# The first unit's expert is chosen before the last unit is routed, and its rows are turned before the table of the others

## The chip, the cores and the metric

The kernel runs on one core of one Trainium2 chip. The time is that of the whole program in device microseconds, the median of the runs shown. The core's engines are TensorE (PE in the rows, with its weight loads as PEld), VectorE (DVE), ScalarE (ACT), GpSimd (POOL) and SyncE (SP), which only starts transfers and reads values. SP and ACT each have a queue of transfers (SPq and ACTq in the rows), and POOL a third one, for transfers whose row numbers come from a tile.

## The reference

Three networks follow each other. An attention over 32 memory slots per head gives 4608 rows of 512. A router sends each row to one of 8 experts, and the expert's result, weighted by the router's probability, is the input of a last dense network.

```python
attn_out = _attn_ref(q, k, v, phi)                      # (8, 8, 576, 64)
x = attn_out.transpose(0, 2, 1, 3).reshape(4608, 512)
logits = x @ w_gate + modality_bias[modality_id]
e_idx = np.argmax(logits, axis=1)
# ... softmax over the logits; gate_w is the probability of the expert taken
for e in range(8):
    mask = e_idx == e
    h = np.maximum(x[mask] @ w1[e], 0.0)                # w1: 512 x 1024
    out[mask] = gate_w[mask, None] * (h @ w2[e])        # w2: 1024 x 512
h = out @ w_in                                          # 512 x 2048
g = np.maximum(h, 0.0) + np.log1p(np.exp(-np.abs(h)))
return g @ w_out                                        # 2048 x 512
```

How many rows an expert gets is known only while the program runs.

## The kernel before

**Attention and routing** (attention_and_routing). The 4608 rows are 18 units of 256 rows. A unit's scores, softmax and values give its rows and router logits. `route` takes the largest logit, and `rank` counts, with matmuls by a triangular matrix, which place each row gets within its expert's region of the array `xs` in memory; the running counts are in `base`. POOL then scatters the rows into `xs`, 128 at a time (L449). Units go to `rank` in pairs, but the last two, 16 and 17, go alone. On each engine the order of this part is made by the framework's scheduler.

**Two choices.** `choose(0)` runs after unit 9 and picks the expert that has the most rows by then; 256 of its rows are read back and computed among the rest of the attention (`chosen`, L481). `choose(1)` runs after the last `rank`: it picks the expert with the most rows left, and 512 of its rows become unit 0 of the expert stage. Both put the expert's number and its first row into the tile `few` (L459, L462), which SP and ACT read with a value load.

**The table** (`listed`, twice, L586 to L643). Some sixty small VectorE instructions on one partition turn the counts into the list of the other units: expert, first row, place of the result. It follows `choose(1)` in the code.

**The expert stage** (experts) is in an order written out by hand. Its head is L746 to L770. ACT starts the first quarter of both weight matrices of unit 0 as soon as the expert is known (L749). SP and ACT start the reading of the 512 rows into `raw` (L752), two transfers each. SP then starts the rest of the weights, the gates `ig` and the first piece of the last network's weights (`convert_in(0)`, tile `d`). `part(0, 0)` and `part(0, 1)` split the first weights into a high and a low half (ACT writes the high one, VectorE the low one), and four calls of `turn` each transpose a quarter of the rows (VectorE) and split it (ACT and VectorE) into `hl`. The unit's loop of 8 steps follows. Step n is 12 matmuls of layer 1 (`hidden_of`, tile `ph`), a relu on ACT and VectorE (`h`, L125 and L126), the splits of weights that later steps need, and 12 matmuls of layer 2, two steps behind. The rows of the unit after it are read into the same `raw` (`rows_of(1)`, by a value of the table) and turned in steps 3 and 4.

What a pool of tiles leaves free when it closes is given to pools that open later. An instruction that writes such a tile waits for everything that used the memory before.

Of the kernel before, what the change touches and what calls it, by code (L numbers as in the profile page):

```python
# [9 lines left out]
F32 = mybir.dt.float32  # L10
# [9 lines left out]
P = 128  # L20
# [3 lines left out]
UNITS = TILES // 2  # L24
DM = H * D
E, F = 8, 1024
FF = 2048
FC = F // P
# [49 lines left out]
def full(tc, *reads):  # L78

    for w in reads:  # L80
        tc.add_to_no_dep_group("full", w.ins)
# [56 lines left out]
def tile_kernel(ctx, tc, qT, kv, phi, mid, wg, mbias, w1, w2, wffn, out):  # L138
# [21 lines left out]
    rows = ExitStack()  # L160
    ps_y = rows.enter_context(tc.tile_pool(name="ps_y", bufs=2, space=PSUM, side="right"))
    ig0 = cst.tile([P, 2, 2], F32, name="ig0")
    weights, py0 = attention_and_routing(tc, locals())
    act = ctx.enter_context(tc.tile_pool(name="act", bufs=1))
    raw = act.tile([P, UNIT // 32, P], F32, name="raw")
# [3 lines left out]
    ids = [act.tile([P, BLK // P], I32, name=f"ids{j}") for j in range(2)]  # L169
    idf = act.tile([P, BLK // P], F32, name="idf")  # L170
    ps_3 = ctx.enter_context(tc.tile_pool(name="ps_3", bufs=2, space=PSUM))
    begun = experts(tc, locals())
    rows.close()
    last_network(tc, locals())
# [2 lines left out]
def attention_and_routing(tc, env):  # L177
    nc = tc.nc
    V, A, G, PE, SP = nc.vector, nc.scalar, nc.gpsimd, nc.tensor, nc.sync
    qT, kv, phi, mid, wg, mbias, w1, w2 = (env[n] for n in ("qT", "kv", "phi", "mid", "wg", "mbias", "w1", "w2"))  # L180
    xs, table, nslots, pick, ig0, ps_y, K, Q, J = (
        env[n] for n in ("xs", "table", "nslots", "pick", "ig0", "ps_y", "K", "Q", "J"))

    with ExitStack() as st:
        pool = lambda name, bufs, **kw: st.enter_context(tc.tile_pool(name=name, bufs=bufs, **kw))
# [25 lines left out]
        iota_i = c.tile([P, TILES], I32, name="iota_i")  # L211
        G.iota(iota_i, pattern=[[P, TILES]], base=0, channel_multiplier=1)
        desc = c.tile([P, E], F32, name="desc")
        base = [c.tile([P, E], F32, name=f"base{i}") for i in range(2)]
        zero_base = c.tile([P, E], F32, name="zero_base")
        for e in range(E):
            G.memset(desc[:, e:e + 1], float(E - e))
            G.memset(base[0][:, e:e + 1], float(e * RG + PAD))
            G.memset(zero_base[:, e:e + 1], float(e * RG + PAD))
        ids = c.tile([P, TILES], F32, name="ids")  # L220
        V.tensor_copy(ids, iota_i)
        zero = c.tile([P, ROW], F32, name="zero")
# [11 lines left out]

        W = Expert(nc, env)
        cnt = [c.tile([1, E], F32, name=f"cnt{i}") for i in range(3)]
        past = [zero_base[0:1], *(c.tile([1, E], F32, name=f"past{i}") for i in range(2))]
        most = c.tile([1, 2], F32, name="most")
        raw0 = lt.tile([P, SLOT // 32, P], F32, name="raw0")
        apart = ["xs"]  # L240
# [185 lines left out]
        def rank(gi):  # L426
# [19 lines left out]
            V.reciprocal(xr[:, 0:n, DM + 1], gs)  # L446
            V.scalar_tensor_tensor(xr[:, 0:n, DM], ri, 0.0, ids[:, t0:t0 + n], op0=ALU.mult, op1=ALU.add)
            for i in range(n):
                once(G.indirect_dma_start(xs, IndirectOffsetOnAxis(ap=ri[:, i:i + 1], axis=0), xr[:, i, :], None,  # L449
                                          bounds_check=E * RG - 1, oob_is_err=False))  # L450

        def choose(i, rows):

# [99 lines left out]
        for u in range(UNITS):  # L553
            if u == 0:
                load(2)
            point(4 * u)
            if u + 2 < UNITS:
                scores(u + 2)
            if u in (0, 2, 5, 7, 9):
                load(3 + (0, 2, 5, 7, 9).index(u))  # L560
            point(4 * u + 1)
            values(u, 0)
            point(4 * u + 2)
            if u + 1 < UNITS:
                transp(u + 1)
            values(u, 1)
            if u and u - 1 == units[group[u - 1]][-1]:
                rank(group[u - 1])
                if u == CHOICE:
                    choose(0, base[(group[u - 1] + 1) % 2][0:1])  # L570
                    fetch()
            if u == units[group[u]][-1]:
                route(group[u])
            point(4 * u + 3)
            if u == CHOICE:
                steps = chosen()
            if u in PADS:
                for e in range(2 * (u - PADS[0]), 2 * (u - PADS[0]) + 2):
                    once(pad(SP, xs, zero, e))
            for i in range(STEPS.get(u, 0)):  # L580
                next(steps)
        rank(len(units) - 1)
        choose(1, base[len(units) % 2][0:1])


        last = base[len(units) % 2][0:1]  # L586
        I = lambda *s, n, dt=F32: c.tile([1, *s], dt, name=n)
        V.memset(table, 1)

# [51 lines left out]
        *_, n = listed(SLOT, MAXS, TABU, n_s, end_s, None)  # L641
        V.tensor_scalar(nslots, n, 1.0 / SLOT, float(SLOTS_E), op0=ALU.mult, op1=ALU.max)
        V.tensor_scalar(nslots, nslots, float(TABU), None, op0=ALU.add)  # L643
        for _ in steps:
            pass
    return W, *chosen_rows


def experts(tc, env):
# [5 lines left out]
    with ExitStack() as st:  # L655
# [87 lines left out]
            regs[s] = value(0, entry(s), E - 1), value(3, entry(s), 1)  # L743

        with tc.manual_schedule():
            head = lambda w, eng, hi: eng.value_load(pick[1][:, w:w + 1], min_val=0, max_val=hi)  # L746
            ea, x0 = head(0, A, E - 1), head(1, SP, E * RG - UNIT)
            for w in range(2):
                load(w, 0, ea, eng=A)  # L749
            xa = head(1, A, E * RG - UNIT)  # L750
            for x, eng, js in ((x0, SP, (0, 1)), (xa, A, (2, 3))):
                full(tc, *rows_in(nc, eng, raw, xs[ds(x, UNIT)], UNIT, js))  # L752
            e0 = head(0, SP, E - 1)
            for w in range(2):
                load(w, 1, e0)
            igs[0], w = gates_in(x0, UNIT)
            full(tc, w)
            for w in range(2):
                load(w, 2, e0)
            convert_in(0)  # L760
            for w in range(2):
                load(w, 3, e0)
            part(0, 0)
            part(0, 1)
            for k in range(4):
                list(turn(1, k, UNIT))
            expert_of(1)
            load(0, 0, *regs[1])
            rows_of(1)
# [223 lines left out]
```

## Time and profile before

| what | value |
|---|---|
| time, median of 3 runs (lowest, highest) | 1412.92 us (1411.44, 1417.55) |
| the profiled execution's own time | 1422.22 us |
| its span, first to last instruction | 1420.2 us |
| PE busy, share of the span | 1370.2 us, 96% |
| DVE, ACT, POOL busy | 922.5, 674.6, 256.9 us |
| mean granted clock of TensorE | 0.976 |

The profiled execution lies 2.0 us above its own span and 9.3 us above the median of the runs. PE's busy share is near 100% through the expert stage and the last network; the slices of the span in which it is lower are the first 150 us, the passage from routing to the expert stage near 182 us, and the passage to the last network near 600 us. Times in the rows are from the span's start.

### The profile page before, as it was taken

Reading aid. Unit: us, or ns where it says so; the run is one execution under the profiler, and the core shown is the slowest. Engines: PE = TensorE matmul, PEld = TensorE weight load, DVE = VectorE, ACT = ScalarE, POOL = GpSimd, SP = SyncE. Lnnn points to the kernel's source line nnn. Section 1 sums busy time; section 2 is a strip of 40 time slices with the busy share of each in tenths; the row PEclk is TensorE's granted clock in tenths of the full one; section 3 lists DMA queues with packets and bytes.
Section 4 is the critical chain, followed back from the end, with each engine's and each line's share of the span. In section 5 each row is a group of like instructions: output and inputs, shape, how many; then the busy total and the mean of one; then the engine's idle time right before and its main releaser. Section 6 shows DMA issues by size and latency. Waiting matters only on the chain.

```text
span 1420.2 us, 19794 instructions
## 1 busy us (share of the span) xinstructions
PE 1370.2 (96%) x7312; PEld 1100.9 (78%) x7312; DVE 922.5 (65%) x1699; ACT 674.6 (48%) x1193; POOL 256.9 (18%) x267
## 2 busy tenths in 40 slices
PE   7997989999999999889999999999999999999997
PEld 5775758878888888668888888888888888888885
DVE  4665857777877775769665756657566575665553
ACT  3554435444443445356544545445454454544443
POOL 1343314333434334300100101001010010100101
PEclk8889989999999999999999999999999999999998
DMA  9975984445334566244010200202001020000000
GB/s 357 402 285 202 374 240 102 104 113 140 95 99 127 170 213 182 89 143 133 23 38 0 60 1 23 38 0 60 1 23 38 0 60 1 23 8 1 30 1 30
DMA packets 94338, 143.03 MB, mean 101 GB/s; under 512 B 16160, under 2 KB 54048, under 8 KB 94240
## 3 DMA queue, kind: packets, MB, share of 16 engines
q1 hardware_dynamic: 86320, 120.94, 28.5%
q0 software_dynamic: 5760, 19.17, 3.5%
q10 hardware_dynamic: 2160, 1.63, 0.4%
q8 instruction: 58, 0.95, 0.3%
q14 instruction: 40, 0.33, 0.1%
HBM read 122.28 MB, written 44.62 MB: 118 GB/s over the span
## 4 chain that ended last, share of the span: by engine, by line
PE 50%; issue 6%; POOL 0%; DMA 0%; ACT 0%; DVE 0%; POOLq 0%; SPq 0%
PE po L67 8%; PE po L69 8%; PE po L68 8%; PE ph L67 8%; PE ph L69 8%; PE ph L68 8%; POOL out L928 0%; DMA s<-wsc 0%; POOLq L989 0%; ACT u L908 0%; DVE g L914 0%; DVE c L913 0%; ACT u L909 0%; ACT g L910 0%; ACT k L58 0%
## 5 line engine op out<-in xcount | busy, mean ns | idle before, releaser
L67 PE MATMUL ph<-hl,k 128*128 128x512 f32 (+1 forms) x536 | 204.3, 381 | 8.2 <-ACT hl L58 5.4
L68 PE MATMUL ph<-hl,k 128*128 128x512 f32 (+1 forms) x536 | 204.3, 381 | 0.0
L58 ACT ACTIVATE gh<-g 128x512 fp32r<-128x512 f32 x144 | 91.0, 632 | 228.3 <-DVE g L915 228.0
L912 DVE TENSOR_SCALAR c<-u 128x512 f32<-128x512 f32 x144 | 61.5, 427 | 194.7 <-ACT u L909 185.2
L928 POOL DMA_INDIRECT out<-ob,ids x36 | 41.3, 1147 | 767.9 <-ACT ob L927 661.7
L69 PE MATMUL ph<-hl,k 128*128 128x512 f32 (+1 forms) x456 | 173.1, 380 | 0.0
L61 DVE TENSOR_TENSOR gl<-g,gh 128x512 fp32r<-128x512 f32 x144 | 99.2, 689 | 84.7 <-ACT gh L58 83.7
L908 ACT ACTIVATE u<-ph 128x512 f32<-128x512 f32 x144 | 86.1, 598 | 133.0 <-PE ph L69 128.1
L67 PE MATMUL py<-q,h 128*128 128x512 f32 x304 | 121.7, 400 | 6.9 <-ACT h L125 5.9
L67 PEld LDWEIGHTS ph<-hl,k 128*128 128x128 f32 x536 | 101.6, 190 | 31.4 <-ACT hl L58 8.2
L69 PE MATMUL py<-q,h 128*128 128x512 f32 x304 | 120.7, 397 | 0.8 <-DVE h L126 0.8
L68 PEld LDWEIGHTS ph<-hl,k 128*128 128x128 f32 x536 | 101.6, 190 | 21.3 <-DVE hl L61 1.8
L126 DVE SCALAR_TENSOR_TENSOR h<-ph,h 128x512 fp32r<-128x512 f32 (+1 forms) x88 | 54.2, 616 | 82.6 <-ACT h L125 82.4
L913 DVE TENSOR_TENSOR c<-c,u 128x512 f32<-128x512 f32 x144 | 99.6, 692 | 4.5
L915 DVE TENSOR_TENSOR g<-g,c 128x512 f32<-128x512 f32 x144 | 99.0, 688 | 4.2
L914 DVE SCALAR_TENSOR_TENSOR g<-ph,g 128x512 f32<-128x512 f32 x144 | 98.3, 684 | 0.9 <-ACT g L910 0.9
L69 PEld LDWEIGHTS ph<-hl,k 128*128 128x128 f32 x456 | 85.7, 188 | 16.3
L125 ACT ACTIVATE h<-ph 128x512 fp32r<-128x512 f32 (+1 forms) x88 | 47.3, 537 | 107.4 <-PE ph L69 101.1
L909 ACT ACTIVATE u<-u 128x512 f32<-128x512 f32 x144 | 90.8, 631 | 4.0
L910 ACT ACTIVATE g<-u 128x512 f32<-128x512 f32 x144 | 90.8, 631 | 3.9
L67 PE MATMUL po<-k,gh 128*128 128x512 f32 x216 | 85.9, 398 | 0.0
L69 PE MATMUL po<-k,gl 128*128 128x512 f32 x216 | 85.5, 396 | 0.0
(236 smaller groups left out, 3083.7 us busy)
## 6 DMA issues: line engine op xcount, KB each, us to landing
k<-w SPq DMA_DIRECT2D x43, 512.0 KB
j<-w SPq DMA_DIRECT2D x43, 512.0 KB
k<-kv SPq DMA_DIRECT2D x36, 512.0 KB
d<-wffn SPq DMA_DIRECT2D x32, 512.0 KB
q<-qT SPq DMA_DIRECT2D x8, 1152.0 KB
raw<-ys SPq DMA_DIRECT2D x36, 256.0 KB
xs<-zero SPq DMA_DIRECT2D x8, 1056.0 KB
ys<-y SPq DMA_DIRECT2D x8, 1026.0 KB
```

The costliest lines, as they stand in the source:

```text
L58: hi_eng.activation(hi, x, AF.Copy)
L61: lo_eng.tensor_tensor(lo, x, hi.bitcast(F32), ALU.subtract)
L67: nc.tensor.matmul(out, lh, rh, start=start, stop=False)
L68: nc.tensor.matmul(out, lh, rl, start=False, stop=False)
L69: nc.tensor.matmul(out, ll, rh, start=False, stop=stop)
L908: A.activation(u, ph, AF.Abs)
L909: A.activation(u, u, AF.Exp, scale=-1.0)
L910: A.activation(g, u, AF.Ln, bias=1.0)
L912: V.tensor_scalar(c, u, 1.0, 1.0, op0=ALU.add, op1=ALU.subtract)
L913: V.tensor_tensor(c, c, u, ALU.subtract)
L914: V.scalar_tensor_tensor(g, ph, 0.0, g, op0=ALU.max, op1=ALU.add)
L915: V.tensor_tensor(g, g, c, ALU.subtract)
```

## The change

`choose(1)` runs after `rank` of unit 16, so its counts leave out the 256 rows of unit 17. A new function `head_and_table` holds the head of the expert stage and, behind it, the table; the expert stage starts with `convert_in(0)`. The last unit's scatters are put in a group named "late", and the reads of unit 0's rows and gates are declared free of that group. All first weights are started by SP, behind the rows; ACT starts none. The tiles `base`, `past` and `ig1` live in a pool that stays open, and the table's tiles in a pool `tab`, which opens after the attention's pools have closed and closes before the expert stage's open.

```diff
     ig0 = cst.tile([P, 2, 2], F32, name="ig0")
+    ig1 = cst.tile([P, UNIT // P, 2], F32, name="ig1")
+    base = [cst.tile([P, E], F32, name=f"base{i}") for i in range(2)]
+    past = [cst.tile([1, E], F32, name=f"past{i}") for i in range(3)]
     weights, py0 = attention_and_routing(tc, locals())
...
     ps_3 = ctx.enter_context(tc.tile_pool(name="ps_3", bufs=2, space=PSUM))
+    head_and_table(tc, locals())
     begun = experts(tc, locals())
...
-                once(G.indirect_dma_start(xs, IndirectOffsetOnAxis(ap=ri[:, i:i + 1], axis=0), xr[:, i, :], None,
-                                          bounds_check=E * RG - 1, oob_is_err=False))
+                w = once(G.indirect_dma_start(xs, IndirectOffsetOnAxis(ap=ri[:, i:i + 1], axis=0), xr[:, i, :], None,
+                                              bounds_check=E * RG - 1, oob_is_err=False))
+                if gi == len(units) - 1:
+                    tc.add_to_no_dep_group("late", w.ins)
...
+                if u == UNITS - 1:
+                    choose(1, base[(group[u - 1] + 1) % 2][0:1])
...
         rank(len(units) - 1)
-        choose(1, base[len(units) % 2][0:1])
-        last = base[len(units) % 2][0:1]
...
+        for _ in steps:
+            pass
+    return W, *chosen_rows
+
+
+def head_and_table(tc, env):
...
+    with tc.tile_pool(name="tab", bufs=1) as c, tc.manual_schedule():
+        head = lambda w, eng, hi: eng.value_load(pick[1][:, w:w + 1], min_val=0, max_val=hi)
+
+        def early(*reads):
+
+            full(tc, *reads)
+            for w in reads:
+                tc.declare_no_dep(w.ins, group="late", reason="disjoint rows")
+
+        x0 = head(1, SP, E * RG - UNIT)
+        xa = head(1, A, E * RG - UNIT)
+        for x, eng, js in ((x0, SP, (0, 1)), (xa, A, (2, 3))):
+            early(*rows_in(nc, eng, raw, xs[ds(x, UNIT)], UNIT, js))
+        e0 = head(0, SP, E - 1)
+        early(SP.dma_start(ig1, xs[ds(x0, UNIT), DM:DM + 2].rearrange("(t p) c -> p t c", p=P)))
+        for i in range(FC // 2):
+            for w in range(2):
+                W.load(w, i, e0)
+        for k in range(4):
+            xt = c.tile([P, UNIT], F32, name="xt", tag="xt", bufs=2)
+            V.transpose(xt.rearrange("p (a b) -> p a b", b=32), raw[:, :, 32 * k:32 * k + 32])
+            split(nc, xt, hl[:, 1, 0, k], hl[:, 1, 1, k], A, V)
+        for n in range(2):
+            W.part(0, n, V)
+        last = base[0][0:1]
...
-            head = lambda w, eng, hi: eng.value_load(pick[1][:, w:w + 1], min_val=0, max_val=hi)
-            ea, x0 = head(0, A, E - 1), head(1, SP, E * RG - UNIT)
-            for w in range(2):
-                load(w, 0, ea, eng=A)
-            xa = head(1, A, E * RG - UNIT)
-            for x, eng, js in ((x0, SP, (0, 1)), (xa, A, (2, 3))):
-                full(tc, *rows_in(nc, eng, raw, xs[ds(x, UNIT)], UNIT, js))
-            e0 = head(0, SP, E - 1)
-            for w in range(2):
-                load(w, 1, e0)
-            igs[0], w = gates_in(x0, UNIT)
-            full(tc, w)
-            for w in range(2):
-                load(w, 2, e0)
+            igs[0] = env["ig1"]
             convert_in(0)
-            for w in range(2):
-                load(w, 3, e0)
-            part(0, 0)
-            part(0, 1)
-            for k in range(4):
-                list(turn(1, k, UNIT))
             expert_of(1)
```

The rows that follow are the order of instructions in the built programs, with the semaphores that each one waits for in brackets. DMASW0 to DMASW7 count POOL's scatters (the last unit's two are counted by DMASW2 and DMASW3), DMAHW0 to DMAHW7 the transfers of SP and ACT; an engine's name stands for its own counter.

SyncE (SP), where the reading of unit 0's rows is started, in the kernel before; `few` is the choice, `raw` the rows, `k` and `j` are first weights:

```order
L746 TENSOR_LOAD few [waits DVE_49]
L746 ISA x2
L51 ISA
L51 DMA raw<-xs 32x16x128 [waits DMASW5_49,DMASW6_49,DMASW4_49,DMASW7_49,DMASW3_49,DMAHW0_49,DMASW2_49,DMAHW3_49,DMASW1_49,DMAHW4_49,DMASW0_49,DMAHW5_49,DVE_49,DMAHW6_49,PE_49,DMAHW7_49,Activation_49,Pool_49]
L51 ISA
L51 DMA raw<-xs 32x16x128 [waits DMAHW1_49]
L746 TENSOR_LOAD few
L746 ISA x2
L102 ISA
L102 DMA k_1742<-w 128x1024 [waits DMAHW2_49]
L102 ISA
L102 DMA j_1746<-w 128x1024
```

The same place in the changed kernel; `d` is the first piece of the last network's weights:

```order
L600 TENSOR_LOAD few [waits DVE_49]
L600 ISA x2
L742 DMA d<-wffn 128x1024 [waits DMASW3_49,DMASW2_49,DMASW4_49,DMASW1_49,DMASW5_49,DMASW0_49,DMASW6_49,DVE_49,DMASW7_49,PE_49,DMAHW4_49,Activation_49,Pool_49]
L51 ISA
L51 DMA raw<-xs 32x16x128 [waits DMAHW5_49,DMAHW3_49,DMAHW6_49,DMAHW2_49,DMAHW7_49,DMAHW1_49,DMAHW0_49]
L51 ISA
L51 DMA raw<-xs 32x16x128
L600 TENSOR_LOAD few
L600 ISA x2
L613 ISA
L613 DMA ig_73<-xs 128x4x2
L102 ISA
```

The transfer of `d` now stands ahead of the rows on this queue, and it is the one that waits for all eight counters of the scatters. In the built program the counts that it waits for on DMASW2 and DMASW3 are those of the last unit's scatters: its tile lies in memory that held the row numbers of these scatters.

ScalarE (ACT), from its half of the rows to its first relu of unit 0, in the kernel before:

```order
L51 ISA
L51 DMA raw<-xs 32x16x128 [waits DMASW6_49,DMASW7_49,DMASW5_49,DMAHW0_49,DMASW4_49,DMAHW3_49,DMASW3_49,DMAHW4_49,DMASW2_49,DMAHW5_49,DMASW1_49,DMAHW6_49,DMASW0_49,DMAHW7_49,DVE_49,Activation_49]
L51 ISA
L51 DMA raw<-xs 32x16x128
L58 ACTIVATE k_1749<-k_1741 128x512 [waits DMAHW1_49]
L58 ACTIVATE k_1749<-k_1741 128x512
L58 ACTIVATE hl<-xt 128x512 [waits DVE_49] x4
L125 ACTIVATE h<-ph 128x512 [waits PE_49,Activation_49]
L58 ACTIVATE q_1738<-j_1745 128x512 [waits DMAHW2_49]
L58 ACTIVATE k_1750<-k_1742 128x512 [waits DMAHW2_49]
```

The same place in the changed kernel:

```order
L51 ISA
L51 DMA raw<-xs 32x16x128 [waits DMASW7_49,DMAHW0_49,DMASW6_49,DMAHW1_49,DMASW5_49,DMAHW2_49,DMASW4_49,DMAHW3_49,DMASW3_49,DMAHW4_49,DMASW2_49,DMAHW5_49,DMASW1_49,DMAHW6_49,DMASW0_49,DMAHW7_49,DVE_49,Activation_49]
L51 ISA
L51 DMA raw<-xs 32x16x128
L58 ACTIVATE hl<-xt 128x512 [waits DVE_49] x4
L58 ACTIVATE k_1750<-k_1742 128x512 [waits DMAHW2_49]
L58 ACTIVATE k_1750<-k_1742 128x512
L125 ACTIVATE h<-ph 128x512 [waits PE_49,DVE_49,Activation_49,Pool_49]
L58 ACTIVATE q_1739<-j_1746 128x512 [waits DMAHW3_49]
L58 ACTIVATE k_1751<-k_1743 128x512 [waits DMAHW4_49]
```

The rows still wait for all eight counters of the scatters, DMASW2 and DMASW3 with the last unit's counts, and `raw` shares 64 bytes of each partition with a tile from which these scatters read. The split of the first weights (`k`) stands behind that of the rows (`hl`). The first relu (`h`) now waits for VectorE and POOL too: its tile lies where the table's tiles were, and the count that it waits for on VectorE is that of the table's last use of them.

VectorE (DVE), from the table's end to the first rows, in the kernel before; `z` is the low half of the first weights:

```order
L642 TENSOR_SCALAR few<-sums_3_2522 1x1
L643 TENSOR_SCALAR few<-few 1x1 [waits DVE_49]
L61 TENSOR_TENSOR z_1753<-k_1741,k_1749 128x512 [waits DMAHW1_49,Activation_49]
L61 TENSOR_TENSOR z_1753<-k_1741,k_1749 128x512 [waits Activation_49]
L675 STREAM_TRANSPOSE xt<-raw 128x512 [waits DMAHW0_49,DMASW7_49,DMAHW1_49,DMASW6_49,DMAHW3_49,DMASW5_49,DMAHW4_49,DMASW4_49,DMAHW5_49,DMASW3_49,DMAHW6_49,DMASW2_49,DMAHW7_49,DMASW1_49,DMASW0_49]
L61 TENSOR_TENSOR hl<-xt,hl 128x512 [waits Activation_49]
L675 STREAM_TRANSPOSE xt<-raw 128x512
L61 TENSOR_TENSOR hl<-xt,hl 128x512 [waits Activation_49]
L675 STREAM_TRANSPOSE xt<-raw 128x512
L61 TENSOR_TENSOR hl<-xt,hl 128x512 [waits Activation_49]
L675 STREAM_TRANSPOSE xt<-raw 128x512
L61 TENSOR_TENSOR hl<-xt,hl 128x512 [waits Activation_49]
```

VectorE around the same four transposes in the changed kernel:

```order
L619 STREAM_TRANSPOSE xt<-raw 128x512 [waits DMAHW0_49,DMASW7_49,DMAHW1_49,DMASW6_49,DMAHW2_49,DMASW5_49,DMAHW3_49,DMASW4_49,DMAHW4_49,DMASW3_49,DMAHW5_49,DMASW2_49,DMAHW6_49,DMASW1_49,DMAHW7_49,DMASW0_49,DVE_49]
L61 TENSOR_TENSOR hl<-xt,hl 128x512 [waits Activation_49]
L619 STREAM_TRANSPOSE xt<-raw 128x512
L61 TENSOR_TENSOR hl<-xt,hl 128x512 [waits Activation_49]
L619 STREAM_TRANSPOSE xt<-raw 128x512
L61 TENSOR_TENSOR hl<-xt,hl 128x512 [waits Activation_49]
L619 STREAM_TRANSPOSE xt<-raw 128x512
L61 TENSOR_TENSOR hl<-xt,hl 128x512 [waits Activation_49]
L61 TENSOR_TENSOR z_1754<-k_1742,k_1750 128x512 [waits DMAHW2_49,Activation_49]
L61 TENSOR_TENSOR z_1754<-k_1742,k_1750 128x512 [waits Activation_49]
L627 MEMSET table 1x92
L673 TENSOR_TENSOR n_u<-base_74,past_78 1x8
```

Before, the whole table stands ahead of the first split of weights and the transposes. Now the table begins (the clearing of `table`) behind the four transposes and that split, with the first relu of the stage behind its end.

## Rows read from the trace of the kernel before

**Rows 1.** by stretches: busy us of PE, PEld, DVE, ACT, POOL; clock, DMA share, GB/s.

```profile
174.00:176.00 2.00, 2.00 (x11) 1.59 (x10) 1.79 (x14) 0.00 (x0) 0.00 (x0) 1.00 0.96 385
176.00:178.00 2.00, 2.00 (x10) 1.64 (x9) 1.70 (x11) 0.00 (x0) 0.00 (x0) 1.00 0.25 101
...
182.00:184.00 2.00, 0.00 (x0) 0.00 (x0) 0.00 (x0) 0.00 (x0) 0.00 (x0) 1.00 1.17 242
...
187.00:195.00 8.00, 7.64 (x13) 3.53 (x14) 4.63 (x7) 2.01 (x4) 0.00 (x0) 0.50 1.03 395
```

**Rows 2.** timeline of PE: start, us, engine, line, what [idle before <- releaser].

```profile
187.17 0.80 PE L67 MATMUL ph<-hl,k 128*128 128x512 f32 x1 [5.42 <-ACT hl L58]
...
194.95 0.63 PE L67 MATMUL ph<-hl,k 128*128 128x512 f32 x1
195.37 0.63 PE L68 MATMUL ph<-hl,k 128*128 128x512 f32 x1
...
199.02 0.39 PE L67 MATMUL ph<-hl,k 128*128 128x512 f32 x1
...
199.48 0.39 PE L69 MATMUL ph<-hl,k 128*128 128x512 f32 x1
```

**Rows 3.** timeline of POOL, the last scatter.

```profile
170.63 0.98 POOL L449 DMA_INDIRECT xs<-xrow,ri  x1 [0.30 <-issue]
```

**Rows 4.** waits of the SP queue, 160 to 200 us: us in total, times, longest.

```profile
SPq L51 <- DMA xs<-xrow,ri: 7.1, 1, 7.1
```

**Rows 5.** transfers by queue, 172 to 178 us: packets, MB, share of 16 engines.

```profile
DMA packets 500, 1.68 MB, mean 280 GB/s; under 512 B 80, under 2 KB 80, under 8 KB 500
...
q10 hardware_dynamic: 286, 1.04, 45.3%
q0 software_dynamic: 182, 0.58, 25.8%
```

**Rows 6.** timeline of ACT and of its queue.

```profile
170.26 0.37 ACTq L102 DMA_DIRECT2D k<-w  x1
...
178.17 1.01 ACTq L51 DMA_DIRECT2D raw<-xs  x2
179.23 1.16 ACT L58 ACTIVATE k<-k 128x512 fp32r<-128x512 f32 x2 [8.17 <-issue]
...
192.52 0.63 ACT L58 ACTIVATE hl<-xt 128x512 fp32r<-128x512 f32 x1 [1.38 <-DVE xt L675]
195.24 0.60 ACT L125 ACTIVATE h<-ph 128x512 fp32r<-128x512 f32 x1 [2.10 <-PE ph L69]
...
196.26 0.62 ACT L58 ACTIVATE k<-k 128x512 fp32r<-128x512 f32 x1
```

**Rows 7.** timeline of the SP queue.

```profile
178.22 0.90 SPq L51 DMA_DIRECT2D raw<-xs  x2
...
183.06 0.39 SPq L706 DMA_DIRECT2D d<-wffn  x1
...
192.51 2.28 SPq L51 DMA_DIRECT2D raw<-xs  x4
```

**Rows 8.** timeline of DVE.

```profile
169.97 0.16 DVE L634 TENSOR_TENSOR n_u<-base,past 1x8 f32<-1x8 f32 x1
...
177.60 0.14 DVE L643 TENSOR_SCALAR few<-few 1x1 int32<-1x1 int32 x1
179.90 1.29 DVE L61 TENSOR_TENSOR z<-k,k 128x512 fp32r<-128x512 f32 x2 [2.16 <-ACT k L58]
185.74 0.71 DVE L675 STREAM_TRANSPOSE xt<-raw 128x512 f32<-128x512 f32 x1 [4.55 <-DMA raw<-xs]
...
196.91 1.36 DVE L61 TENSOR_TENSOR k<-k,k 128x512 fp32r<-128x512 f32 x1 [0.35 <-ACT k L58]
...
205.52 1.29 DVE L675 STREAM_TRANSPOSE xt<-raw 128x512 f32<-128x512 f32 x2
```

**Rows 9.** one line: the clearing of `sums`; ns min/median/max, first and last start.

```profile
L595 DVE MEMSET sums<- x8: 78/78/78, 1.6 to 1.9; 1x24 f32 x8
```

More of the change, by code (lines that the diff above doesn't have):

```diff
@@ L180, in attention_and_routing @@
     qT, kv, phi, mid, wg, mbias, w1, w2 = (env[n] for n in ("qT", "kv", "phi", "mid", "wg", "mbias", "w1", "w2"))
-    xs, table, nslots, pick, ig0, ps_y, K, Q, J = (
-        env[n] for n in ("xs", "table", "nslots", "pick", "ig0", "ps_y", "K", "Q", "J"))
+    xs, pick, ig0, ps_y, base, past, K, Q, J = (env[n] for n in ("xs", "pick", "ig0", "ps_y", "base", "past", "K", "Q", "J"))
     with ExitStack() as st:
@@ L213, in attention_and_routing @@
         desc = c.tile([P, E], F32, name="desc")
-        base = [c.tile([P, E], F32, name=f"base{i}") for i in range(2)]
-        zero_base = c.tile([P, E], F32, name="zero_base")
         for e in range(E):
@@ L218, in attention_and_routing @@
             G.memset(base[0][:, e:e + 1], float(e * RG + PAD))
-            G.memset(zero_base[:, e:e + 1], float(e * RG + PAD))
+            G.memset(past[0][:, e:e + 1], float(e * RG + PAD))
         ids = c.tile([P, TILES], F32, name="ids")
@@ L236, in attention_and_routing @@
         cnt = [c.tile([1, E], F32, name=f"cnt{i}") for i in range(3)]
-        past = [zero_base[0:1], *(c.tile([1, E], F32, name=f"past{i}") for i in range(2))]
         most = c.tile([1, 2], F32, name="most")
@@ L582, in attention_and_routing @@
         rank(len(units) - 1)
-        choose(1, base[len(units) % 2][0:1])
-        last = base[len(units) % 2][0:1]
+        for _ in steps:
+            pass
+    return W, *chosen_rows
+def head_and_table(tc, env):
+    nc = tc.nc
+    V, A, G, PE, SP = nc.vector, nc.scalar, nc.gpsimd, nc.tensor, nc.sync
+    xs, table, nslots, pick, raw, hl, ig1, W, base, past = (
+        env[n] for n in ("xs", "table", "nslots", "pick", "raw", "hl", "ig1", "weights", "base", "past"))
+    with tc.tile_pool(name="tab", bufs=1) as c, tc.manual_schedule():
[20 more added lines that the diff above has]
+        last = base[0][0:1]
         I = lambda *s, n, dt=F32: c.tile([1, *s], dt, name=n)
@@ L643, in attention_and_routing @@
         V.tensor_scalar(nslots, nslots, float(TABU), None, op0=ALU.add)
-        for _ in steps:
-            pass
-    return W, *chosen_rows
 def experts(tc, env):
```

## The prediction, made before the changed kernel was run

> **What bounds the kernel now.** I read the view by stretches first. PE is busy throughout the expert stage and the last network, so a change at one passage is worth what PE loses there. In the passage from routing to expert stage PE does nothing from 182 to 184 us, and from 187 to 195 us it runs at a granted clock of 0.50, the lower of its two levels of 1.2 and 2.4 GHz [rows 1]. The timeline of PE gives the wait a name: 5.42 us for ACT's `hl`, the first quarter of unit 0's rows, until 187.17 us [rows 2]. The first 12 matmuls of layer 1 then go at the pace of the four turns of rows until 194.95, the next 12 until 199.02, and from there PE is continuous [rows 2].
>
> Going back from 187.17: the first transpose starts at 185.74, after VectorE sat idle 4.55 us for the rows [rows 8]. Their reading was started at 178.17 on ACT's queue and 178.22 on SP's [rows 6, 7], and SP had waited 7.1 us for the scatters [rows 4]. The last scatter started at 170.63 on POOL [rows 3]. So the chain is: last scatter, 7.5 us until the reading starts, 7.57 us until the first transpose, 1.43 us to PE. The table is nowhere in it: it runs on VectorE from 169.97 to 177.74 [rows 8], while PE finishes the early expert and the scatters land.
>
> **The change part by part.**
>
> *The choice made earlier.* It is meant to let the reading start before the last scatters land. The built order says otherwise: both halves of the reading still wait for the last unit's counts, ACT's by itself and SP's behind `d`. I count no gain here. Nine one-partition VectorE instructions stand ahead of the last `rank` instead of behind it; at 0.16 us each, as the table's first [rows 8], they can delay the last scatter by 0 to 1.4 us. Most fall into gaps between dependent steps; I take 0.2. POOL's two index fills stand ahead of unit 16's scatters, which have slack to the last ones: 0.
>
> *ACT's early weights are gone.* Before, ACT starts the first weights at 170.26, eight microseconds ahead of the rows [rows 6]. Between 172 and 178 us its queue (q10) moves 1.04 of 1.68 MB, the scatters' queue (q0) 0.58 [rows 5]. The DMA engines are full until 176 [rows 1], so the last scatter stands in a crowd. Without q10, 0.64 MB are left; at 385 GB/s [rows 1] that is 1.7 us, and the landing could come near 173.7 instead of just before 178.2. The ends are 0 and 4.5 us gained. I take 3.4, nearer to the full gain, since most of the bytes go, but the last stretch, at a DMA share of only 0.25 [rows 1], is a tail that fewer bytes don't shorten. The Trainium skill ("DMA: Bandwidth & Descriptors", section "Queues, rings and completion order") says that each DMA engine takes turns between the queues it has work for. By that rule q10's weights cost the scatters their turns, and the gain is real; if scatters had their own way to memory, it would be 0 and the sum 8.9 instead of 5.5.
>
> *`d` ahead of the rows on SP.* Issuing it takes 0.39 us [rows 7], and its bytes, as many as each of the two weights on q10 (0.52 MB, [rows 5]), are read beside the rows: 1.4 us at 385 GB/s if all of it comes first. Ends 0.4 and 1.8; I take 1.2. The same section of the skill says that descriptors of one queue are consumed in ring order on each engine, a rule that speaks against this placing: by it SP's half of the rows stands behind all of `d`, the upper end. ACT's half is on another queue, so I stay below that end.
>
> First transpose: 185.74 + 0.2 - 3.4 + 1.2 = 183.7.
>
> *Turns first, then the weights' split.* PE no longer goes quarter by quarter: the split of the first weights stands behind the four turns on ACT. The last high half of rows ends at 192.52 + 0.63, that is 7.41 us after the first transpose [rows 6, 8]. One split of 0.6 us later, at 8.0 us after it (191.7), PE can start. Twelve matmuls at 0.42 us [rows 2] are 5.1 us, twelve more about 4.1 us (194.95 to 199.02): PE would be ready for the third group at 200.9. That alone is +1.9 us. The weights themselves are no limit: started near 178, they have 13 us, and before they had at most 9 (170.26 to 179.23) among full engines [rows 6].
>
> *The table behind all that.* This is the main term. Before, the table is hidden; now it begins when the low halves of the weights are done. From the start of the high halves to the end of the low ones is 179.23 to 181.19, 1.96 us [rows 6, 8]; so it begins at 183.7 + 7.41 + 1.96 = 193.1. Its length before is 7.8 us with one relu of 0.4 in it, so 7.4 alone. The clearing of `sums` adds 0.3 (eight starts from 1.6 to 1.9, [rows 9]), the clearing of the table and two casts about as much, and code order, in which dependent steps follow each other, some more: I take 8.4, ends 7.4 and 9.5. It ends at 201.5.
>
> *The relu that waits for the table.* ACT's first `h` waits for VectorE's count at the table's end. Behind it on ACT, which takes its instructions in order, stands everything PE needs next: the high half of the weights of the third group. Before, that split started 1.02 us after the first relu (195.24, 196.26), and VectorE's low half ended 3.03 us after it (196.91 + 1.36) [rows 6, 8]. So the third matmul of the third group can go at 201.5 + 3.0 = 204.5, where it went at 199.48 [rows 2]: +5.0 us. Layer 2 and the splits behind it follow in the old spacing. PE stands for about 3 us before this group; in the stretch before, a gap of 5.42 us ended with the clock at the low level [rows 1, 2]. I add 0.5 for it, ends 0 and 2.
>
> *Unit 1's rows* need the table's first list. They were read from 192.51 and turned at 205.52 [rows 7, 8]. Now the list is done about 4 us into the table, the reading starts near 198 to 200 and, at 7.6 us like unit 0's, is in by 207.6, while its place on VectorE has moved to 205.5 + 5 = 210.5. Covered by 3 us; without that cover VectorE would hold the relus behind it.
>
> Sum: +5.5 us, from +2.0 (4.5 gained, 0.4, 7.4, no clock) to +11.9 (nothing gained, 1.8, 9.5, 2). The profiled execution would go from 1422.22 to 1427.7. That execution lies 9.3 above the median shown; the same difference on the median gives 1412.92 + 5.5 = 1418.4.
>
> **The rivals.** What a measurement here can tell from no change is 0.5%, 7.1 us.
>
> *A. It does what it says.* The reading starts without the last scatters, and the table hides. The best case is a reading that starts when the last scatter is only issued, 171.6; first transpose 179.2, PE at 187.2 as now, but then 12 matmuls in a row until 192.3 instead of 194.95: -2.7 us, 1410.2. For it speaks that the reads are declared free of the last scatters; against it the waits in the built order, on the rows and on the first relu. Chance 0.07, and even then it is no measurable gain.
>
> *B. The scatters land no earlier* (the slower side). If the last scatter's 7.5 us are its own and not the crowd's, the first transpose comes at 187.1, the table ends at 204.9, the third group's weights are ready at 207.9: +8.4, with a longer stand of PE and its clock +9.4, 1422.3. It decides from the point where less than 1.8 us are gained, a reading that starts after 176.6. For it speaks the tail at share 0.25 [rows 1]; against it q10's 1.04 MB [rows 5]. Chance 0.28.
>
> *C. Unit 1's rows come late.* If their reading takes over 10.5 us instead of 7.6, the cover is gone and VectorE stalls before the relu of step 3; two to four microseconds more, 1421. Chance 0.08.
>
> **How the numbers follow.** My forecast keeps 0.57, a hundredth of it for what I don't see, with its own range of +2 to +8 (1415 to 1421); nearly all of it lies within 0.5%. Same: 0.52 of it, 0.06 of A, 0.03 of C, 0.61. Slower: 0.04 of it, 0.28 of B, 0.05 of C, 0.37. Faster: 0.01 of A and that hundredth, since no case worked out here reaches 7 us. The range takes in A's edge and B: 1412 to 1424.
>
> **What would show it.** Right: the reading starts after the last scatter's landing, near 175; a first transpose near 184; the table's first instruction after the fourth turn; ACT's first 128x512 relu waiting for VectorE; PE idle once from 181 to about 192 and again before the third group. Wrong in the large: a reading that starts before 172, or a first relu that doesn't wait for the table. If the reading starts at 178 as before, B is right.

## The result, and the profile after

The changed kernel takes 1421.62 us (median of 14 runs, 1416.14 to 1423.5), the kernel before 1412.57 beside it (14 runs, 1409.6 to 1417.55). The ratio is 1.0058, 95% interval 1.0045 to 1.0070: slower by 6 to 10 us. The forecast was 1418.4 and its likeliest case "within 0.5%"; the time lies inside the range, and the ratio just beyond that bound, which the interval (1.0045 to 1.0070) straddles.

The execution shown ahead of the prediction was slower than others of the same kernel in its own attention: its last scatter started at 170.63 us [rows 3], in five other executions of kernels with the same attention between 145.6 and 154.9. So another profiled execution of the kernel before (1414.99 us, span 1412.9) is the fair one to hold against the changed kernel's (1422.44 us, span 1420.4). Their last scatters start at 151.86 and 151.53. All differences below are between these two, unless another kernel is named.

Timelines of POOL, SP, ACT, VectorE and PE in that second execution of before (start, us, engine, line, what, idle before):

```profile
151.86 0.98 POOL L449 DMA_INDIRECT xs<-xrow,ri  x1 [0.30 <-issue]
170.55 0.90 SPq L51 DMA_DIRECT2D raw<-xs  x2
177.57 0.71 DVE L675 STREAM_TRANSPOSE xt<-raw 128x512 f32<-128x512 f32 x1 [4.06 <-DMA raw<-xs]
179.00 0.80 PE L67 MATMUL ph<-hl,k 128*128 128x512 f32 x1 [16.30 <-ACT hl L58]
190.66 0.39 PE L69 MATMUL ph<-hl,k 128*128 128x512 f32 x1
193.13 0.60 ACT L125 ACTIVATE h<-ph 128x512 fp32r<-128x512 f32 x1 [1.09 <-PE ph L69]
```

The same in the changed kernel:

```profile
151.53 0.98 POOL L449 DMA_INDIRECT xs<-xrow,ri  x1 [0.30 <-issue]
159.52 0.35 SPq L742 DMA_DIRECT2D d<-wffn  x1
167.64 0.88 SPq L51 DMA_DIRECT2D raw<-xs  x2
174.33 0.71 DVE L619 STREAM_TRANSPOSE xt<-raw 128x512 f32<-128x512 f32 x1 [21.97 <-DMA ig<-xs]
182.31 0.80 PE L67 MATMUL ph<-hl,k 128*128 128x512 f32 x1 [19.87 <-DMA j<-w]
183.62 0.14 DVE L627 MEMSET table<- 1x92 int32 x1
192.70 0.14 DVE L682 TENSOR_SCALAR few<-few 1x1 int32<-1x1 int32 x1
192.78 0.60 ACT L125 ACTIVATE h<-ph 128x512 fp32r<-128x512 f32 x1 [10.01 <-DVE few L681]
194.47 0.57 PE L67 MATMUL ph<-hl,k 128*128 128x512 f32 x1 [3.81 <-ACT k L58]
195.86 0.80 PE L69 MATMUL ph<-hl,k 128*128 128x512 f32 x1 [0.39 <-DVE k L61]
199.52 0.60 ACT L125 ACTIVATE h<-ph 128x512 fp32r<-128x512 f32 x1 [2.42 <-PE ph L69]
```

Three things are to be seen. The reading of the rows (`raw`) starts 2.9 us earlier, but still 16.1 us after the last scatter starts. The table (183.62 to 192.84) stands behind the turns, and ACT's first relu `h`, idle for 10.01 us, is released by its end. Some 5 of these 10 us PE's first 12 matmuls take anyway (with the table first, below, the same relu waits 5.11 us for PE alone); the other 5 are the table's. And the third relu, from which the units run in the old spacing, comes 6.4 us later than before (199.52 against 193.13).

Stretches of the changed kernel (busy us of PE, PEld, DVE, ACT, POOL; clock; DMA share; GB/s), which answer to [rows 1]:

```profile
168.00:182.00 14.00, 0.00 (x0) 0.00 (x0) 4.88 (x8) 2.78 (x5) 0.00 (x0) 0.50 1.02 334
182.00:191.00 9.00, 8.35 (x24) 6.27 (x24) 8.14 (x56) 0.77 (x2) 0.00 (x0) 0.67 0.42 137
191.00:195.00 4.00, 0.53 (x2) 0.30 (x2) 2.91 (x10) 2.22 (x5) 1.02 (x1) 0.97 1.19 230
195.00:199.00 4.00, 3.61 (x11) 2.53 (x10) 2.86 (x3) 2.10 (x4) 2.17 (x3) 0.60 0.47 145
```

PE stands twice, until 182.31 and from 190.7 to 194.5, and its clock falls twice: to 0.50 in the long gap, and again to 0.60 on average right behind the second one, at the lower of the two levels (1.2 and 2.4 GHz) for most of 195 to 199. The 6.4 stays to the last relu of the expert stage (598.2 against 591.8). The spans differ by 7.5; the other 1.1 us fall into the 820 us of the last network, and no wait of the trace stands for them.

### The profile page after: what moved, and what is told of

Read it like the earlier page. It is cut to its first block, busy times and chain, and to the rows that moved or that the text cites. A ratio compares the mean times of both kernels' runs of the same rounds, so it can differ in the third digit from the quotient of the medians.

```text
span 1420.4 us, 19793 instructions
## 1 busy us (share of the span) xinstructions
PE 1362.2 (96%) x7312; PEld 1096.2 (77%) x7312; DVE 925.7 (65%) x1699; ACT 674.3 (47%) x1193; POOL 255.3 (18%) x267
## 4 chain that ended last, share of the span: by engine, by line
PE 51%; issue 6%; ACT 0%; POOL 0%; POOLq 0%; ACTq 0%
PE po L67 8%; PE po L69 8%; PE ph L68 8%; PE po L68 8%; PE ph L69 8%; PE ph L67 8%; POOL out L945 0%; ACT u L925 0%; POOLq L1006 0%; ACT u L926 0%; ACT g L927 0%; ACT k L58 0%; POOLq L945 0%; ACTq L837 0%; ACTq L925 0%
```

## The experiments

**The kernel before once more.** A second profiled execution, without an edit.

> The kernel before, unchanged, for a second profile. In its first one the last scatter starts at 170.63 us, in that of the changed kernel at 151.5, although nothing of the change stands in that stretch. Theory E (that execution was slow in its attention by itself): here the last scatter starts between 150 and 156 us, the cleared pads are through near 168 to 172 and set the start of the rows' reading, and the third group of layer 1 of unit 0 starts near 190 us; span 1408 to 1415. Theory F (the change itself shortens the attention by some 19 us): here the last scatter starts at 168 to 172 us again, the third group at 198 to 200, span 1418 to 1422.

1414.99 us: the last scatter starts at 151.86 us, so the slow attention belonged to that first execution. It also opens a question that the prediction had not seen: here the reading starts 18.7 us after the last scatter, not 7.5.

**The table first.** In `head_and_table` the four turns and the split of the first weights are moved behind the table.

```diff
-        for k in range(4):
-            ...   # transpose and split of a quarter of the rows
-        for n in range(2):
-            W.part(0, n, V)
         last = base[0][0:1]
         ...
         V.tensor_scalar(nslots, nslots, float(TABU), None, op0=ALU.add)
+        for k in range(4):
+            ...
+        for n in range(2):
+            W.part(0, n, V)
```

> The changed kernel with one part undone: in the code of the head the table stands ahead of the four turns and the split of the first weights again. Theory T (the table on VectorE behind the turns, with ACT's first relu waiting for it, holds PE before the third group): the table is done while the rows arrive, PE starts unit 0 as in the changed kernel, but the third group follows at once, 4 to 5 us earlier; about 1417 us against 1421.6. Theory D (the loss lies in how late the rows and first weights arrive): no change, 1420 to 1423.

1415.69 us (10 runs) beside 1415.12 for before, ratio 1.0001 (0.9986 to 1.0016). The whole loss is gone, more than was expected. VectorE, SP and ACT of this kernel:

```profile
158.39 0.14 DVE L676 TENSOR_SCALAR few<-few 1x1 int32<-1x1 int32 x1
167.15 0.88 SPq L51 DMA_DIRECT2D raw<-xs  x2
187.28 0.60 ACT L125 ACTIVATE h<-ph 128x512 fp32r<-128x512 f32 x1 [5.11 <-PE ph L69]
193.02 0.60 ACT L125 ACTIVATE h<-ph 128x512 fp32r<-128x512 f32 x1 [1.38 <-PE ph L69]
```

The table now ends at 158.5, while PE still computes the early expert, and the first relu waits for PE alone.

**The table in memory of its own.** The order of the code stays; the table's tiles become slices of scratch tiles of the pool `b_cv`, which opens earlier, so that `h` takes over none of their memory.

```diff
-        I = lambda *s, n, dt=F32: c.tile([1, *s], dt, name=n)
+        room, used = [env["cv"].tile([P, 512], I32, name=f"room_{t}", tag=t) for t in "abc"], [0, 0, 0]
+        def I(*s, n, dt=F32):
+            ...   # a slice of one of the three, behind what is used
```

> The changed kernel with the table's tiles in memory that nothing else uses until unit 1 (the scratch of the weights' conversion) instead of memory that the first relu's tile takes over; code order unchanged. In the built order the table then mixes with the relus and splits of the first steps on VectorE, and ACT's first relu waits for PE and one transpose alone. Theory T: the third group starts 3 to 5 us earlier, about 1417 us. Theory D: no change, 1420 to 1423. If VectorE's sheer work for the table is what counts and not the wait, a gain of 1 us or less.

1414.62 us, ratio 1.0008 (0.9991 to 1.0024). SP's reading, ACT's relus and the end of the table:

```profile
161.66 0.89 SPq L51 DMA_DIRECT2D raw<-xs  x2
181.26 0.60 ACT L125 ACTIVATE h<-ph 128x512 fp32r<-128x512 f32 x1 [4.41 <-PE ph L69]
187.78 0.60 ACT L125 ACTIVATE h<-ph 128x512 fp32r<-128x512 f32 x1 [2.17 <-PE ph L69]
193.10 0.14 DVE L696 TENSOR_SCALAR few<-few 1x1 int32<-1x1 int32 x1
```

The table still runs in this passage, to 193.24, but the first relu no longer waits for it (181.26): in the built program the relus and splits stand between its instructions on VectorE. From the start of the reading to the third relu it takes 26.1 us here (187.78 less 161.66), 25.9 with the table first, 31.9 in the changed kernel, 22.6 in before. So VectorE's work for the table is nearly free there; what cost 6 us was that `h` took over the table's memory and had to wait for its last instruction, on ACT and, as the relu's second half stands behind the table there, on VectorE. The edit lifts both together, so no run tells these two apart.

**Before, with the first weights behind the rows.** The other part of the change by itself.

```diff
-            ea, x0 = head(0, A, E - 1), head(1, SP, E * RG - UNIT)
-            for w in range(2):
-                load(w, 0, ea, eng=A)
+            x0 = head(1, SP, E * RG - UNIT)
...
-            for w in range(2):
-                load(w, 1, e0)
+            for i in range(2):
+                for w in range(2):
+                    load(w, i, e0)
```

> The kernel before with one part of the change alone: the first quarter of unit 0's weights is started by SP behind the rows, not by ACT ahead of them. Theory Q (these 1.04 MB hold up whatever must land before the rows are read): the reading starts 2 to 3 us earlier and the time falls to about 1410. Theory W (the first weights are needed early): ACT's split of them, which stands ahead of the rows' split in this kernel, waits for them, and the time rises by 1 to 5 us, 1414 to 1418.

1412.78 us, ratio 0.9987 (0.9972 to 1.0003). The reading starts at 171.15, 16.3 us after this execution's last scatter (154.90) instead of 18.7; but ACT then waits until 178.79 for the weights. Gained and given back.

The second number is the clue: some 16 us after the last scatter, whatever the order. What SP's queue still moves until 167 us are the eight clearings of the regions' first 512 rows (`pad`, called for units 11 to 14), 1056 KB or 1.08 MB each, which the reads of `xs` wait for too. The waits of the SP queue in the changed kernel, 150 to 170 us, name them (us in total, times, longest):

```profile
SPq L742 <- DMA xs<-xrow,ri: 7.8, 1, 7.8
SPq L51 <- DMA xs<-zero: 7.4, 1, 7.4
```

The scatters are waited for by `d`, which is given out at 159.52; the rows then wait 7.4 us more, for the clearings. The next three kernels give the clearings out three units earlier.

**The clearings earlier**, in the table-first version, in before and in the changed kernel, with the same edit:

```diff
-PADS = range(11, 15)
+PADS = range(8, 12)
```

> The table-first version of the changed kernel, with the eight clearings of the pads (8 x 1.06 MB on SP's queue) given out three units earlier (units 8 to 11 instead of 11 to 14), where the DMA engines are busy at 0.2 to 0.6 only. Theory G (the clearings, not the last scatters, hold the reading of unit 0's rows): the reading starts at 159 to 161 us, right behind the last scatter, instead of 167.2; first transpose 166 to 167.5 instead of 173.7; PE starts 173 to 175 instead of 181.7; the time falls by 6 to 9 us, ratio to the kernel before 0.994 (1404 to 1409). Rival H (the last scatters or the queue's own latency hold it): the reading starts at 165 or later, the time stays at 1413 to 1416, ratio 0.998 to 1.001. Rival L (the earlier clearings hold up the last loads of the attention): the early expert's last relu comes 2 us or more later and eats the gain.

> The kernel before with nothing changed but the clearings of the pads three units earlier. Theory G: reading starts at 159 to 161 instead of 170.6, and since the table lies beside the early expert as before, the gain is whole: 8 to 10 us, ratio 0.993 to 0.994 (1403 to 1407), without any of the change under study. Theory A (the earlier choice is what lets the reading come early): reading not before 165, gain under 3 us. Rival L as above: no gain.

> The changed kernel with nothing changed but the clearings of the pads three units earlier. Theory G: the reading starts at 159 to 161 instead of 167.6, but the table stays behind the turns and the split: table from about 175 to 184.5, ACT's first relu waits for its end for 8 to 10 us as before this edit; so it gains 7 to 8 us on the changed kernel and comes to 1413 to 1416, ratio to the kernel before 0.999 to 1.001. Theory A: the reading starts before the last scatter has landed, at 157 or earlier, and the ratio falls below 0.997.

All three are slower: 1432.28, 1428.86 and 1439.31 us beside 1422.97 for before in these runs; ratios 1.0062 (1.0039 to 1.0085), 1.0042 (1.0024 to 1.0060) and 1.0097 (1.0073 to 1.0121). The forecast of a gain failed through rival L. SP's queue, a stretch (columns as above), the last scatter, the table's next-to-last instruction and a wait of the SP queue, in before with early clearings:

```profile
96.92 25.59 SPq L74 DMA_DIRECT2D xs<-zero  x3
110.00:120.00 10.00, 10.00 (x100) 7.37 (x95) 3.67 (x18) 2.97 (x5) 2.71 (x4) 0.50 0.16 56
127.53 1.92 SPq L51 DMA_DIRECT2D raw<-xs  x4
175.69 0.98 POOL L449 DMA_INDIRECT xs<-xrow,ri  x1 [0.30 <-issue]
183.60 0.13 DVE L642 TENSOR_SCALAR few<-sums 1x1 int32<-1x1 f32 x1
183.98 0.89 SPq L51 DMA_DIRECT2D raw<-xs  x2
SPq L51 <- DVE few L642: 4.7, 1, 4.7
```

and in the changed kernel with them:

```profile
178.58 0.97 POOL L449 DMA_INDIRECT xs<-xrow,ri  x1 [0.30 <-ACT h L125]
182.41 0.88 SPq L51 DMA_DIRECT2D raw<-xs  x2
210.63 0.60 ACT L125 ACTIVATE h<-ph 128x512 fp32r<-128x512 f32 x1 [10.01 <-DVE few L681]
```

The attention itself comes late. In before with early clearings the DMA engines are full from 100 to 110 us (a share of 1.04, where the second execution of before has 0.26), PE runs at a granted clock of 0.50 from 110 to 120 (there 1.00 from 110 to 118), the early expert's rows are given out from 127.53 (there from 116.21), and the last scatter comes 21 to 27 us late in the three. What each of these costs was not taken apart.

For theory G this is no test. With scatters this late the clearings are through before them wherever they stand: in the first execution of before, with the clearings in their old place, the reading followed a late scatter by only 7.5 us too. What the three kernels show instead is a third wait. In the table-first version and in the changed kernel the reading starts 3.8 us after the last scatter, in before 8.3 us after it, and there the profile names the table as what ended the wait: 4.7 us for `few`, written by the table's next-to-last instruction. So in the kernel before the rows also wait for the table, which is not seen as long as it ends before scatters and clearings do.

**Some clearings later.** Of the eight, four (or two) are given out by SP behind unit 0's weights; nothing ahead of the routing's end moves.

```diff
-PADS = range(11, 15)
+PADS = range(11, 13)        # with two late ones: range(11, 14)
...
             for w in range(2):
                 W.load(w, i, e0)
+        for e in range(4, E):   # with two late ones: range(6, E)
+            w = SP.dma_start(xs[e * RG:e * RG + PAD]..., env["zeros"]...)
```

> The table-first version of the changed kernel with four of the eight clearings of the pads as before (units 11 and 12) and four given out by SP behind unit 0's weights. 4.2 MB less stand on SP's queue ahead of unit 0's rows, and the early expert's rows and weights keep their place. Theory G (the clearings hold the reading of unit 0's rows): the attention keeps its times, the reading starts at 158.5 to 161 us instead of 167.2, first transpose 165 to 167.5 instead of 173.7, PE 173 to 175 instead of 181.7; of these 7 to 8 us up to 3 may go to unit 1's rows, which now stand behind the late clearings; ratio to the kernel before 0.994 to 0.997. Rival H (the last scatters or the queue's latency hold the reading): start at 165 or later, ratio 0.998 to 1.001. Rival L2 (the late clearings hold unit 1's rows so long that VectorE and the relus behind it stand): reading early, ratio 1.000 or more.

> The same with two of the eight clearings late. Theory G: the six early ones end 2.1 MB, some 5.5 us, sooner, so that the reading starts at 160 to 163 us, and unit 1's rows are held less; ratio 0.995 to 0.998. Rival H: as with four, start at 165 or later, 0.998 to 1.001.

> The changed kernel itself (turns and split ahead of the table) with four clearings late. Theory G: reading at 155 to 161 us, that is 6 to 12 earlier than in the changed kernel; the table stays behind the turns, ACT's first relu waits 8 to 10 us for its end; ratio to the kernel before 0.998 to 1.001, 5 us or more slower than the table-first version. If the choice ahead of the last routing is worth something once the clearings are out of the way, the reading starts before the last scatter has landed (before 158 us) and 1 us or more earlier than in the table-first version only if the table there holds it; otherwise at the same time.

Beside 1414.52 for before: table first with four late 1411.08, ratio 0.9980 (0.9965 to 0.9994); with two late 1409.77, 0.9967 (0.9949 to 0.9985); the changed kernel with four late 1412.89, 0.9979 (0.9961 to 0.9997). Table first, four late:

```profile
153.36 0.98 POOL L450 DMA_INDIRECT xs<-xrow,ri  x1 [0.30 <-issue]
158.13 0.88 SPq L51 DMA_DIRECT2D raw<-xs  x2
192.10 0.63 ACT L58 ACTIVATE k<-k 128x512 fp32r<-128x512 f32 x1 [6.23 <-DMA k<-w]
198.35 1.30 DVE L718 STREAM_TRANSPOSE xt<-raw 128x512 f32<-128x512 f32 x2 [4.90 <-DMA raw<-xs]
```

Two late:

```profile
150.91 0.97 POOL L450 DMA_INDIRECT xs<-xrow,ri  x1 [0.30 <-issue]
162.22 0.88 SPq L51 DMA_DIRECT2D raw<-xs  x2
169.57 0.71 DVE L686 STREAM_TRANSPOSE xt<-raw 128x512 f32<-128x512 f32 x1 [10.92 <-DMA ig<-xs]
188.86 0.60 ACT L125 ACTIVATE h<-ph 128x512 fp32r<-128x512 f32 x1 [1.11 <-PE ph L69]
```

The changed kernel, four late:

```profile
151.56 0.98 POOL L450 DMA_INDIRECT xs<-xrow,ri  x1 [0.30 <-issue]
156.71 0.88 SPq L51 DMA_DIRECT2D raw<-xs  x2
182.78 0.60 ACT L125 ACTIVATE h<-ph 128x512 fp32r<-128x512 f32 x1 [10.01 <-DVE few L688]
```

Theory G is shown, by scatters that keep their times: with 4.3 MB less ahead of the rows the reading starts 4.8 and 5.1 us after the last scatter, with 2.2 MB less 11.3 after it. Rival H fell. With four late the longest wait of SP's queue ahead of the rows (5.7 and 6.1 us) is again that for the scatters. One more thing differs there: `d` is now given out near 180 us, behind the rows; with two late it is ahead of them as before (158.71).

With four late and the table first more than half goes back at once, and the ratio of 0.9980 misses the 0.994 to 0.997 of the expectation: the reading is some 11 us earlier than in the table-first version by its distance from the last scatter, the expert stage's last relu 2.1 (589.6 against 591.7, with scatters that came 2.6 later): 4.7 in all. ACT waits 6.23 us for weights of a later step and VectorE 4.90 for unit 1's rows, which stand behind the late clearings.

In the changed kernel the relu's wait for the table is 10.01 us still, the same number as without the edit: earlier rows don't shorten it. The expected distance of 5 us to the table-first version did not show in the times (1412.89 against 1411.08, intervals that overlap). The traces say why: counted from the last scatter the table-first version leads by 7.0 us at the third relu (184.23 against 189.38) and by 0.3 at the last (589.64 against 588.10), for the weights that come late hold it as much as the table holds the other.

**The best version tried**: two clearings late, table first, the first weights split between the turns, unit 1's rows turned one step later.

```diff
             split(nc, xt, hl[:, 1, 0, k], hl[:, 1, 1, k], A, V)
-        for n in range(2):
-            W.part(0, n, V)
+            if k < 2:
+                W.part(0, k, V)
...
-                    k = n - (3 if s == 0 else 0)
+                    k = n - (4 if s == 0 else 0)
```

> The table-first version with two clearings late, and two more edits: the two splits of the first weights go between the turns (behind the first and the second of the four) instead of behind all of them, and unit 1's first rows are turned one step of unit 0 later. Theory W (turns ahead of the weights' split cost PE some 3 us, as the third group of layer 1 came 16.1 us after the first transpose with the table first, and 12.6 in the kernel before): PE starts 3 to 4.5 us after the first transpose instead of 8.0, the third group comes 12.5 to 14 us after it, VectorE no longer waits 2 us for unit 1's rows; 2 to 4 us better than with two late clearings alone, ratio to the kernel before 0.994 to 0.996 (1406 to 1408 beside 1414). Rival (the first weights land too late for it, since they are read behind the rows): ACT waits for the weights and with them the second turn; PE starts no earlier than 7 us after the first transpose, ratio as with two late clearings alone, 0.996 to 0.998.

1408.96 us (12 runs) beside 1414.93, ratio 0.9963 (0.9949 to 0.9976). VectorE, PE and ACT:

```profile
166.41 0.71 DVE L686 STREAM_TRANSPOSE xt<-raw 128x512 f32<-128x512 f32 x1 [10.89 <-DMA ig<-xs]
168.36 0.80 PE L67 MATMUL ph<-hl,k 128*128 128x512 f32 x1 [9.68 <-ACT k L58]
183.79 0.60 ACT L125 ACTIVATE h<-ph 128x512 fp32r<-128x512 f32 x1 [1.11 <-PE ph L69]
```

PE starts 1.95 us after the first transpose, where theory W expected 3 to 4.5; the third group starts 14.4 us after it (180.84), just outside the expected 12.5 to 14; and the third relu comes 17.4 us after it, where two late clearings alone have 19.3 (169.57 to 188.86). The 1.9 us are in the trace; the times of the two (0.9963 and 0.9967) don't tell them apart, so the forecast gain of 2 to 4 us between them is not shown. It beats both kernels: by some 5 us on before by the ratio, about 13 on the changed kernel by the two ratios.

## Why the prediction was right and where it was wrong

**The choice made earlier: 0 was right.** The reading still starts 16.1 us after the last scatter, and in before with the weights late, which chooses after the last routing, 16.3. With the clearings out of the way it waits for the last scatters all the same (4.8 and 5.1 us with four late, 3.8 with all early), as the built order said. The 8.3 us of before with early clearings are no price of the later choice: 4.7 of them are, by the profile, the wait for the table. No run frees the reading of the last scatters, so what that would be worth stays open.

**"The last scatter stands in a crowd": the wait was named wrongly, and the size came out nearly right by luck.** The reading came 2.6 us earlier relative to the last scatter, where 3.4 was taken. But what was held up by ACT's early weights was not the scatters' landing: it was the last clearing on SP's queue. Transfers by queue from 156 to 161.8 us, while these weights move, in the second execution of before:

```profile
q10 hardware_dynamic: 280, 1.03, 43.5%
q1 hardware_dynamic: 395, 0.82, 36.4%
```

and in the changed kernel, which has no q10 there:

```profile
q1 hardware_dynamic: 885, 1.82, 85.8%
```

Beside q10's 1.03 MB SP's queue (q1) moved 1.0 MB less. At the 397 GB/s that all queues together moved in before from 152 to 167 us, the weights' 1.05 MB are 2.6 us (an estimate), which is what was measured; and before with the weights late, 16.3 in place of 18.7, shows it without the rest of the change. The Trainium skill ("DMA: Bandwidth & Descriptors", section "Queues, rings and completion order") has each DMA engine take turns between its queues, and the trace agrees: with q10 at work SP's queue kept moving, but 0.82 MB in place of 1.82. I had read the order of events from an execution in which the scatters came so late, at 170.63 [rows 3], that the clearings were nearly done; there the scatter was the last thing waited for. The 0.64 MB and the tail from which the 3.4 was worked out belong to that execution alone. The same holds for "the table is nowhere in it": there it had ended 0.4 us before the reading, and with early clearings it was what the reading waited for.

**`d` ahead of the rows: 1.2 taken, about 0 measured.** It is given out at 159.52, while the rows still wait for the clearings until 167.64, so it is nearly through by then and takes nothing from them: from reading to first transpose it takes 6.7 us against 7.0 before. With that the first transpose comes 3.2 us earlier, not 2.0.

**Turns first, then the split: right.** Foretold was PE's start 8.0 us after the first transpose; it is 7.98 (174.33 to 182.31), before 1.43 (177.57 to 179.00). From the start of the reading to the third relu the table-first version takes 25.9 us, before 22.6: 3.3 us, as much as the earlier reading gives. That is why the table-first version comes out even.

**The table: mechanism right, size 0.8 short.** It begins 9.29 us after the first transpose (9.4 foretold) and lasts 9.22 us (8.4 taken, bounds 7.4 and 9.5).

**The relu that waits: right.** From the table's end to the third group's third matmul 3.02 us (3.0 foretold), and this matmul comes 5.2 us later than before (+5.0 foretold; 195.86 against 190.66).

**The clock: 0.5 taken, 1.2 measured** from there to the third relu (+6.4 in place of +5.2), since this group starts at the low level: its matmuls follow each other at 0.43 us until 197.7 and at 0.23 behind it, in before at 0.23 throughout. The further microsecond to the end has no place in the trace and stays open.

**The rivals.** A (it does what it says) and C (unit 1's rows late) did not happen. B's time, 1422.3, is near the measured one, but its mechanism is not what the trace shows: it needs a reading less than 1.8 us earlier, and it was 2.6 to 2.9.

**The sum: right in its main terms, and in part by luck.** For the third group's third matmul +5.0 was forecast and +5.2 came, because errors cancel. The first transpose came 1.2 us earlier than the sum had it (`d` cost nothing); the table with its two ends took 0.8 longer; and in the second execution of before this matmul stands 13.1 us behind the first transpose (177.57 to 190.66), not 13.7 as in the execution that the sum was built on, which makes the change 0.6 dearer. What the sum lacked against the 7.5 us of the spans is the clock's 0.7 and the 1.1 us behind the expert stage; by the ratio of the runs the change costs 8.2. (The sum's upper end, +11.9, leaves out the 1.4 us by which its own count lets the scatters be late; nothing hung on it.) That put the likeliest case on the wrong side of the bound.

## What to carry to other kernels

Before a read is moved ahead, ask for every writer of what it reads, not only the one that ends last by program order: here a bulk clearing on the same queue held the rows for 7.4 us after the wait for the scatters, which the change was meant to avoid, had ended. Work that moves into a pool whose memory is handed on makes the next user wait for its last instruction, however little it computes; giving it other memory, or the old place in the order, brought the 6 us back. And look at a second profiled execution before building a chain of waits on one.

## What the runs showed of the hardware that was not expected

A 10.01 us wait of ACT for the table came out the same to the hundredth in three kernels whose rows were read at 167.6, 182.4 and 156.7 us: the passage from the last split to the relu is fixed by VectorE's chain alone. Giving out the 8.7 MB of clearings three units earlier, towards a stretch in which the DMA engines are busy at 0.26 (100 to 110 us) and 0.43 (110 to 118), delayed the last scatter by 21 to 27 us. With it came full DMA engines from 100 to 110, a granted clock of 0.50 from 110 to 120 in two of the three kernels, and the early expert's 256 rows given out 11.3 us later in before (127.53 against 116.21); how the delay divides among them is not shown.
